# Another order for the opening of an mLSTM-and-feed-forward kernel: later gates loaded second, state copies moved, eight filler products less

## The chip, the cores and the metric

The kernel runs on one core of a Trainium2 chip. Its engines are TensorE (PE, with its weight loads shown as PEld), VectorE (DVE), ScalarE (ACT) and GpSimd (POOL); SyncE (SP) issues most of the transfers. The metric is the device time of one launch in microseconds (us), median of several runs. Before the change it is 528.15 us, the median of three runs from 528.1 to 528.36.

## The reference, cut to what matters

Float32 throughout. An mLSTM cell runs over 768 time steps for 4 batches of 8 heads with 40 dimensions each; its output, reshaped to 3072 rows of 320, passes through a feed-forward block with a gated cosine.

```python
for t in range(S):
    m_new = maximum(f_gate[t] + m, i_gate[t])
    f_stab, i_stab = exp(f_gate[t] + m - m_new), exp(i_gate[t] - m_new)
    C = f_stab * C + i_stab * outer(v[t], k[t])      # 40 x 40 for each head
    n = f_stab * n + i_stab * k[t]
    y[t] = sigmoid(o_gate[t]) * (C @ q[t]) / maximum(abs(n . q[t]), 1)
x = y, as (3072, 320)
h = x @ w_in                                         # (320, 2048)
out = (h * cos(h)) @ w_out                           # (2048, 320)
```

## The kernel before, in words

**Chunks and cells.** The time axis is cut into 6 chunks of 128 steps. A *cell* is one chunk of one batch, n = 4c + b, 24 in all (in the code B is 4, C is 128). Within a cell the recurrence is done by products: a 128 x 128 matrix of decays E for each of 8 heads is multiplied into the scores q.k, and that weighs the values; across chunks a state `st[b]` is carried. Once the four cells of a chunk are done, their outputs stand turned in `xT[c]`, and the feed-forward of these 512 rows can begin: class `Up` (L691 for two blocks of 128 features, L697 for the last 64, kept in `w_in_l`), then `near` (ACT L705), `rest` (DVE L708), `sin` (ACT L713) and `gate` (DVE L717) make h cos h, and the products of L729 and L812 go down through `w_out`.

**Order.** Every engine works through its queue in the order in which the program issues, and the order of the opening is written out by hand in `first_cells`: cells 0 to 3 (all of chunk 0), plus the preparation of cell 4, called B. Then `first_parts(b)` interleaves the cells 4 to 7 with the feed-forward of chunk 0, and `both_parts` goes on so for the later chunks.

**Steps of a cell in the opening.** `load` and `load_E` issue transfers on SP. `wall_in` and `spread` (PE) or, for cells 2 and 3, a load of rows of M from DRAM give the exponents; `decay_exponents` subtracts the gate sums (DVE L415, for halves L421) and for the cells whose E was loaded masks the upper triangle (POOL L416); `decay` is the exponential (ACT L426, L430). `turn` transposes queries and keys (PE L462), `scores` multiplies them (PE L523), `weigh` multiplies scores by E (DVE L529), `values` multiplies with the values (PE L541), `normalize` divides by the denominator (DVE L597 to L605) and leaves y. `weigh_k` (POOL L435) weighs the keys, `seam_u` (PE L652) makes the state's increment `pu` of them, `state` copies it into `st[b]` in four copies (ACT L671), `seam_x` transposes y (PE L637, L639) and `seam_out` copies it into xT (ACT L663). `turn_keys`, `keys_out`, `turn_blocks`, `scale_q` and `odd_values` prepare cell B, whose turned form runs later through `turn_gate` (DVE L501, which transposes the output gate `og` made by `sigmoid(1)`, ACT L338 and L340), vt (PE L554) and `normalize_turned` (DVE L576 to L588).

**Gates.** The gates of chunk 0 (F0, a0) are loaded by `gates_in` and scanned by `gates_first`. The later chunks' gates (F1, a1, 80 KB each) are loaded by `later_gates_in` (L231, L232) and scanned by `gates_sums` (DVE L256), `gates_less_sums` (L259 to L261) and `gates_maxima` (L264, which stores to `M_d[1]`). `gates_exponents` (POOL L271, L272), `gates_exp` (ACT L276, with two POOL stores to `G_d`), `gates_diagonal` (DVE L283), `gates_turn` (PE L291, L292) and `gates_keep` (ACT L297, L300) put the later chunks' gates into the tables `tab` and `fades`.

**Weights.** w_in and w_out come as pairs of 32-bit words that are taken apart on ACT (`take_apart`, L160 and L162) and put together on DVE and POOL (`put_together`, DVE L167, L169, L171, POOL L172), a piece at a time; `pieces` holds those of w_in (a first and a second block of 128 rows, then w_in_l), `outs` those of w_out.

**Fillers.** `warm(k)` issues k products of a zero tile on PE (L895) that nothing reads.

**Tiles.** In the first four cells the PSUM tiles of even cells come from a pool of two buffers (`ps_a`), those of odd cells from one of four (`ps_o`); `ps_u` has two for the two halves of an Up; E has three buffers, so that E(B) takes the buffer of E(0). The tile y and its helper have one buffer each.

Of the kernel before, what the change touches and what calls it, by code (L numbers as in the profile page):

```python
# [29 lines left out]
def kernel(  # L30
# [20 lines left out]
    nc = tc.nc  # L51
# [352 lines left out]
    def psum_o():  # L404
        return ps_o.tile([128, HP, C], FP, name="pm", tag="o")
# [256 lines left out]
            xT[c] = p2.tile([128, NK + 1, B, C], FP, name="xT", tag="xT")  # L662
        nc.scalar.copy(out=xT[c][:, :, b], in_=pxs[n])  # L663

    def state(n):
        if n < N - B:
            for j, r, s, w in halves(n):
                u = increment(n, r, w)
                s = like(s, u)
                if n < B:  # L670
                    nc.scalar.copy(out=s, in_=u)  # L671
                else:
                    nc.vector.tensor_tensor(out=s, in0=s, in1=u, op=OP.add)

# [228 lines left out]
    def first_cells():  # L903
        gates_in()
        nc.scalar.copy(out=ident_b, in_=ident)
        load(0, "qk")
        gates_first()
        fill_raw()
        later_gates_in()
        load(0, "v")  # L910
        load(1, "qk")
        load_o(0, (0, 1))
        load(1, "v")
        load(2, "qk")
        load_E(0)
        load_E(1)
        load_E(2)
        load(2, "v")
        load_E(3)
        load_o(0, (2, 3))  # L920
        load(3)
        pieces.extend(weights_in(0))
        load_two(B, "qk")
        warm(9)
        gates_sums()
        wall_in(0, 1, psum_o())
        wall_in(0, 0, pmu)
        gates_less_sums()
        gates_maxima()
        gates_first_out()  # L930
        turn(0)
        gates_exponents()
        wall_in(1, 0, psum_o())
        spread(0, 0)
        spread(0, 1)
        turn_out(0, False)
        decay_exponents_half(0, 0)
        scores(0)
        decay_exponents_half(0, 1)
        turn(1)  # L940
        decay(0)
        weigh(0)
        spread(1, 0)
        fill_states()
        turn_out(1, False)
        wall_in(1, 1, psum_o())
        decay_exponents_half(1, 0)
        spread(1, 1)
        sigmoid(0, slice(0, 2))
        decay_exponents_half(1, 1)  # L950
        weigh_k(0)
        fill_vr()
        values(0)
        scores(1)
        normalize(0)
        turn(2)
        decay(1)
        decay_exponents(2)
        turn_out(2, False)
        warm(1)  # L960
        seam_u(0)
        load_one(B)
        state(0)
        seam_x(0)
        seam_out(0)
        scores(2)
        weigh(1)
        decay_exponents(3)
        decay(2)
        weigh(2)  # L970
        values(1)
        normalize(1)
        gates_exp()
        load_E(B)
        outs.append((0, weights_out(0)))
        load_E(B + 1)
        load_o(1)
        decay(3)
        turn(3)
        turn_out(3)  # L980
        gates_diagonal()
        sigmoid(0, slice(2, 4))
        values(2)
        seam_x(1)
        seam_out(1)
        take_apart(*pieces[0])
        weigh_k(2)
        scores(3)
        take_apart(*pieces[1])
        normalize(2)  # L990
        take_apart(*pieces[2])
        gates_keep(*gates_turn())
        warm(3)
        weigh(3)
        values(3)
        weigh_k(1)
        seam_u(2)
        seam_x(2)
        seam_out(2)
        put_together(*pieces.pop(0))  # L1000
        pieces.extend(weights_in(1))
        normalize(3)
        seam_u(1)
        load_one(B + 1)
        outs.append((1, weights_out(1)))
        low_dimensions(B)
        seam_x(3)
        seam_out(3)
        turn_keys(B, ps_o, "o")
        keys_out(B)  # L1010
        weigh_k(3)
        put_together(*pieces.pop(0))
        decay_exponents(B)
        turn_blocks(B)
        put_together(*pieces.pop(0))
        state(2)
        seam_u(3)
        decay(B)
        state(1)
        state(3)  # L1020
        weigh_k(B)
        odd_values(B)
        scale_q(B)
        clear_low()
# [21 lines left out]
    def first_parts(b):  # L1046
        n = B + b
        for i in range(2):
# [7 lines left out]
            if i == 0:  # L1056
                scores(n)
                if b == 0:
                    warm(8, psum_o())
                for e in range(2):  # L1060
                    up.near(e)
                for e in range(2):
                    up.rest(e)
                weigh(n)
                if b > 0:
                    decay_exponents(n + 1)
                for e in range(2):
                    up.sin(e)
                if b == 1:
                    take_apart(*pieces[0])  # L1070
                take_apart(*outs[0][1])
                if b == 0:
                    for e in range(2):
                        up.gate(e)
                    turn_blocks(n + 1)
                    next_out()
                    decay_exponents(n + 1)
                    sigmoid(1)
                else:
                    for step in "gw" if b == 1 else "wg":  # L1080
                        if step == "g":
                            for e in range(2):
                                up.gate(e)
                        elif pieces:
                            put_together(*pieces.pop(0))
                            more()
                    next_out()
                    decay(n + 1)
                down_slot(0, f2)
                turn_gate(n)  # L1090
                values(n)
                seam_u(n)
                fade(n)
                normalize_turned(n)
                low_out(n)
                if n == 2 * B - 1:
                    load_two(n + 3, "qk")
                if n > B + 1:
                    load_E(n + 3)
                if b == B - 2:  # L1100
                    load_o(2)
                sin_next()
                if b > 0:
                    if pieces:
                        take_apart(*pieces[0])
                        put_together(*pieces.pop(0))
                        more()
                        take_apart(*pieces[0])
                    take_apart(*outs[0][1])
            else:  # L1110
                if n == 2 * B - 1:
                    load_two(n + 3, "Kv")
                for e in range(2):
                    up.near(e)
                if b == 0:
                    for piece in pieces[0:2]:
                        take_apart(*piece)
                    put_together(*pieces.pop(0))
                    more()
                for e in range(2):  # L1120
                    up.rest(e)
                if b == 0:
                    put_together(*pieces.pop(0))
                    more()
                    load_two(n + 2, "Kv")
                else:
                    state(n)
                for e in range(2):
                    up.sin(e)
                    up.gate(e)  # L1130
                weigh_k(n + 1)
                odd_values(n + 1)
                if b == 0:
                    take_apart(*pieces[0])
                    take_apart(*outs[0][1])
                if b == 0:
                    state(n)
                if pieces:
                    put_together(*pieces.pop(0))
                    if b == 0:  # L1140
                        load_two(n + 2, "q")
                    more()
                if n == B + 1:
                    low_dimensions(n + 1)
                if b == 0:
                    decay(n + 1)
                else:
                    turn_blocks(n + 1)
                    if b < B - 1:
                        turn_keys(n + 1)  # L1150
                        keys_out(n + 1)
                next_out()
                scale_q(n + 1)
                down_slot(0, f2)
                if b == 0:
                    turn_keys(n + 1)
                    keys_out(n + 1)
                    hold(9)
                if b == 1:
                    load_two(n + 3)  # L1160
                if b < 2:
                    load_E(n + 3)
                if b == 1:
                    take_apart(*pieces[0])
                if b == B - 1:
                    weight_sums(0)
# [110 lines left out]
```

## Time and profile before

| what | value |
|---|---|
| median of three runs | 528.15 us (528.1 to 528.36) |
| profiled execution, its time | 527.42 us |
| profiled execution, its span | 525.5 us |
| PE busy | 511.2 us |
| DVE busy | 413.0 us |
| ACT busy | 284.4 us |
| POOL busy | 248.2 us |
| granted PE clock | 1.00 |

The span is the time from the first to the last instruction of the profiled execution; 1.92 us lie around it, and that execution is 0.73 us shorter than the median. The busy times add up to more than the span because the engines run beside one another. In a line of a timeline the first number is the start in us from the span's start, the second is how long the group took, "x8" is how many instructions it groups, and the bracket tells how long the engine had been idle and what it had waited for. In a line of the waits the numbers are the total, how often, and the longest.

The opening, by stages of 5 us, with the busy time of each engine in it:

| stage, us | PE | DVE | ACT | POOL |
|---|---|---|---|---|
| 5 to 10 | 5.00 | 4.09 | 2.25 | 0.63 |
| 10 to 15 | 5.00 | 3.77 | 3.61 | 4.85 |
| 15 to 20 | 4.22 | 4.40 | 4.64 | 3.34 |
| 20 to 25 | 4.98 | 3.25 | 4.46 | 3.89 |
| 25 to 30 | 5.00 | 4.79 | 4.36 | 0.36 |
| 30 to 35 | 4.19 | 4.13 | 3.15 | 2.29 |
| 35 to 40 | 4.48 | 3.28 | 4.72 | 3.55 |
| 40 to 45 | 3.95 | 2.58 | 4.87 | 3.10 |
| 45 to 50 | 5.00 | 4.21 | 4.95 | 0.98 |
| 50 to 55 | 5.00 | 4.86 | 4.42 | 3.98 |
| 55 to 60 | 3.93 | 4.92 | 4.18 | 3.25 |

### The profile page before, as it was taken

How to read it: one execution, taken by the hardware profiler on the slowest of the kernel's cores; microseconds unless marked ns; L12 is line 12 of the kernel's file. 1: busy time of each engine (PE TensorE's matmuls, PEld its weight loads, DVE VectorE, ACT ScalarE, POOL GpSimd, SP SyncE). 2: the span in 40 equal slices, each digit the busy share in tenths (PEclk: the TensorE clock that was granted, in tenths of full speed). 3: DMA queues.
4: the chain of work that ended last, by engine and by line, in shares of the span. 5: the costliest groups of instructions: out<-in, count | busy, mean ns of one | idle time of the engine just before them, and what ended most of it. 6: DMA issues, size and time to landing. Idle time of an engine off the chain costs nothing.

```text
span 525.5 us, 10532 instructions
## 1 busy us (share of the span) xinstructions
PE 511.2 (97%) x3864; PEld 342.4 (65%) x3864; DVE 413.0 (79%) x921; ACT 284.4 (54%) x540; POOL 248.2 (47%) x398
## 2 busy tenths in 40 slices
PE   9999899999999999999999999999999999999996
PEld 6864455555666667666766666676576676666756
DVE  5887998986887887897887898788798878664636
ACT  4979897773953654752652843644745531322221
POOL 6745665544587687355356344444434334121211
PEclk9999999999999999999999999999999999999999
DMA  8898998999266475266357167348110000000001
GB/s 165 212 242 202 282 207 224 181 248 164 95 138 102 97 159 77 71 158 104 97 116 121 53 133 147 85 99 150 41 57 6 1 6 6 26 25 1 0 1 50
DMA packets 96978, 57.15 MB, mean 109 GB/s; under 512 B 62272, under 2 KB 89008, under 8 KB 96928
## 3 DMA queue, kind: packets, MB, share of 16 engines
q1 hardware_dynamic: 95152, 54.66, 48.2%
q0 software_dynamic: 1392, 1.48, 1.2%
q8 instruction: 30, 0.49, 0.4%
q10 hardware_dynamic: 384, 0.36, 0.2%
q14 instruction: 20, 0.16, 0.1%
HBM read 51.05 MB, written 4.11 MB: 105 GB/s over the span
## 4 chain that ended last, share of the span: by engine, by line
PE 79%; ACT 9%; DVE 7%; DMA 2%; issue 2%; POOL 0%; ACTq 0%; SPq 0%; DVEq 0%; POOLq 0%
PE pup L691 28%; PE acc L812 22%; PE pup L697 8%; PE po L729 4%; PE ps L523 3%; PE late L812 2%; ACT E L430 2%; DMA o<-in_o_gate_dram 2%; DVE n L708 1%; PE ph L541 1%; PE pu L652 1%; PE vt L554 1%; ACT L430 1%; ACT L338 1%; PE vt L567 1%
## 5 line engine op out<-in xcount | busy, mean ns | idle before, releaser
L691 PE MATMUL pup<-xT,w_in_sb 128*128 128x512 f32 x384 | 175.8, 601 | 2.5 <-DVE g L717 2.5
L705 ACT ACTIVATE n<-pup 128x512 int32<-128x512 f32 x96 | 53.8, 595 | 195.2 <-PE pup L697 135.3
L708 DVE SCALAR_TENSOR_TENSOR n<-pup,n 128x512 f32<-128x512 f32 x96 | 63.2, 687 | 82.3 <-ACT n L705 80.7
L691 PEld LDWEIGHTS pup<-xT,w_in_sb 128*128 128x128 f32 x384 | 69.7, 190 | 88.8 <-issue 80.3
L771 POOL TENSOR_TENSOR D<-g 128x128 f32<-128x128 f32 x40 | 19.6, 490 | 152.8 <-DVE g L717 138.6
L713 ACT ACTIVATE n<-n 128x512 f32<-128x512 f32 x96 | 59.3, 630 | 14.0 <-DVE n L708 14.0
L717 DVE SCALAR_TENSOR_TENSOR g<-pup,n 128x512 f32<-128x512 f32 x96 | 62.1, 683 | 1.8 <-ACT n L713 0.2
L812 PE MATMUL acc<-w_out_sb,g 128*128 128x160 f32 x320 | 58.5, 304 | 0.0
L812 PE MATMUL acc<-T,g 128*128 128x160 f32 x320 | 57.9, 301 | 0.1
L697 PE MATMUL pup<-xT,w_in_l 64*128 64x512 f32 x192 | 54.3, 641 | 0.5 <-POOL w_in_l L172 0.5
L812 PEld LDWEIGHTS acc<-w_out_sb,g 128*128 128x128 f32 x320 | 47.9, 190 | 5.4 <-issue 3.9
L812 PEld LDWEIGHTS acc<-T,g 128*128 128x128 f32 x320 | 48.2, 190 | 3.4 <-issue 2.7
L430 ACT ACTIVATE E<-E,tab 128x128 f32<-128x128 f32 x160 | 49.0, 388 | 0.4 <-POOL E L416 0.2
L729 PE MATMUL po<-w_out_sb,g 128*128 128x320 f32 x128 | 36.4, 437 | 1.3 <-POOL w_out_sb L172 1.3
L812 PE MATMUL acc<-T,S 128*128 128x160 f32 x160 | 34.9, 300 | 0.0
L589 POOL TENSOR_TENSOR yt<-yt,db 128x128 f32<-128x128 f32 x20 | 11.1, 553 | 48.5 <-DVE db L584 48.5
L523 PEld LDWEIGHTS ps<-t,t 40*128 40x128 f32 (+1 forms) x384 | 25.2, 188 | 11.6 <-issue 7.4
L529 DVE TENSOR_TENSOR E<-ps,E 128x512 f32<-128x512 f32 x48 | 30.7, 681 | 2.0 <-ACT E L426 1.1
L729 PEld LDWEIGHTS po<-w_out_sb,g 128*128 128x128 f32 x128 | 23.7, 190 | 12.3 <-POOL w_out_sb L172 1.7
L697 PEld LDWEIGHTS pup<-xT,w_in_l 64*128 64x128 f32 x192 | 14.6, 185 | 24.1 <-issue 20.8
L812 PE MATMUL acc<-w_out_sb,S 128*128 128x160 f32 x160 | 28.8, 299 | 0.0
L812 PEld LDWEIGHTS acc<-T,S 128*128 128x128 f32 x160 | 26.3, 190 | 2.7 <-issue 2.7
(192 smaller groups left out, 905.9 us busy)
## 6 DMA issues: line engine op xcount, KB each, us to landing
E<-M_d SPq DMA_DIRECT2D x22, 512.0 KB
qr<-in_q_dram SPq DMA_DIRECT2D x36, 160.0 KB
G<-G_d SPq DMA_DIRECT2D x20, 256.0 KB
bits<-in_moe_w_out_dram SPq DMA_DIRECT2D x8, 640.0 KB
kr<-in_k_dram SPq DMA_DIRECT2D x32, 160.0 KB
bits<-in_moe_w_in_dram SPq DMA_DIRECT2D x32, 128.0 KB
out_dram<-o_sb SPq DMA_DIRECT2D x22, 160.0 KB
o<-in_o_gate_dram SPq DMA_DIRECT2D x40, 80.0 KB
```

What stands on the lines that cost most here:

```text
L430: nc.scalar.activation(out=Es[n][:, h], in_=Es[n][:, h], func=AF.Exp, scale=-1.0, bias=tab[:, c, 0, g:g + 1])
L523: nc.tensor.matmul(ps[j][:, p], kT[r, p], qT[r, p], start=True, stop=True)
L529: nc.vector.tensor_tensor(out=w, in0=pss[n][j], in1=w, op=OP.mult)
L691: nc.tensor.matmul(pu, w_in_sb[:, i, ts(2 * f2 + e, 128)], x(i), start=(i == 0 and not low_first), stop=(i == NK - 1 and low_first))
L697: nc.tensor.matmul(pu, w_in_l[r, f2], x(NK, r), start=low_first, stop=not low_first)
L705: nc.scalar.activation(out=self.n[e], in_=self.pu[e], func=AF.Copy, bias=0.25)
L708: nc.vector.scalar_tensor_tensor(out=self.n[e].bitcast(FP), in0=self.pu[e], scalar=0.25, in1=self.n[e], op0=OP.add, op1=OP.subtract)
L713: nc.scalar.activation(out=r, in_=r, func=AF.Sin, scale=TWO_PI_DOWN)
L717: nc.vector.scalar_tensor_tensor(out=g, in0=self.pu[e], scalar=TWO_PI, in1=self.n[e].bitcast(FP), op0=OP.mult, op1=OP.mult)
L729: nc.tensor.matmul(po[c][b], gs[c, f][:, ts(b, C)], w_out_sb[:, f], start=(f == 0), stop=(f == NF - 1))
L771: tt(out=D1, in0=G0[:, 1, 1], in1=G1[:, 1, 1], op=OP.add)
L812: nc.tensor.matmul(a, lhs, rhs, start=start, stop=stop)
```

## The change

No arithmetic changes and no tile changes. `state` takes the copying instruction as an argument, and the steps of `first_cells` are written in another order:

- SP issues the loads of F1 and a1 second and third, ahead of the queries and keys of cell 0; the rest of its order is as it was.
- DVE runs the later gates' scans before it does anything for cell 0's decays, and has decay_exponents(2) ahead of normalize(0) and weigh(1); in the order before it came behind normalize(0).
- POOL has weigh_k(0) and weigh_k(1) before the states are filled, weigh_k(2) ahead of the conversion of the first weights and weigh_k(3) between the first and the second piece; the mask of E(B) (decay_exponents(B)) precedes the additions (L172) of w_in's second piece and of w_in_l, where it stood between them.
- ACT runs the gates' exponentials right behind decay(1), gates_keep ahead of the first take_apart, and takes w_in_l apart ahead of w_in's second piece. Of the twelve state copies L671 that stood between seam_out(3) and near, those of cell 1 come right behind seam_out(1), those of cell 2 go to DVE, and those of cell 3 come in `first_parts`, behind half a piece of w_out and ahead of sigmoid(1).
- PE issues spreads, turns, scores and seams in another order, and 4 fillers in place of 12 besides the nine at the start (warm(1), warm(3), warm(8) become warm(1), warm(3)).

```diff
-    def state(n):
+    def state(n, copy=nc.scalar.copy):
...
-                    nc.scalar.copy(out=s, in_=u)
+                    copy(out=s, in_=u)
...
         gates_in()
         nc.scalar.copy(out=ident_b, in_=ident)
+        later_gates_in()
         load(0, "qk")
         gates_first()
         fill_raw()
-        later_gates_in()
...
         gates_sums()
+        gates_less_sums()
+        gates_maxima()
         wall_in(0, 1, psum_o())
         wall_in(0, 0, pmu)
-        gates_less_sums()
-        gates_maxima()
+        gates_exponents()
+        spread(0, 1)
         gates_first_out()
+        spread(0, 0)
+        decay_exponents_half(0, 0)
         turn(0)
-        gates_exponents()
+        decay_exponents_half(0, 1)
+        wall_in(1, 1, psum_o())
+        spread(1, 1)
         wall_in(1, 0, psum_o())
-        spread(0, 0)
-        spread(0, 1)
+        spread(1, 0)
         turn_out(0, False)
-        decay_exponents_half(0, 0)
+        weigh_k(0)
+        weigh_k(1)
+        fill_states()
+        decay(0)
         scores(0)
-        decay_exponents_half(0, 1)
+        decay_exponents_half(1, 0)
         turn(1)
-        decay(0)
         weigh(0)
-        spread(1, 0)
-        fill_states()
-        turn_out(1, False)
-        wall_in(1, 1, psum_o())
-        decay_exponents_half(1, 0)
-        spread(1, 1)
         sigmoid(0, slice(0, 2))
         decay_exponents_half(1, 1)
-        weigh_k(0)
-        fill_vr()
+        turn_out(1, False)
+        decay(1)
         values(0)
+        gates_exp()
         scores(1)
+        decay_exponents(2)
         normalize(0)
         turn(2)
-        decay(1)
-        decay_exponents(2)
         turn_out(2, False)
-        warm(1)
+        seam_x(0)
         seam_u(0)
         load_one(B)
-        state(0)
-        seam_x(0)
-        seam_out(0)
-        scores(2)
-        weigh(1)
-        decay_exponents(3)
-        decay(2)
-        weigh(2)
-        values(1)
-        normalize(1)
-        gates_exp()
         load_E(B)
         outs.append((0, weights_out(0)))
+        weigh(1)
+        gates_diagonal()
+        values(1)
         load_E(B + 1)
         load_o(1)
+        seam_out(0)
+        state(0)
+        decay_exponents(3)
+        normalize(1)
+        fill_vr()
+        decay(2)
+        scores(2)
+        turn(3)
         decay(3)
-        turn(3)
+        weigh_k(2)
+        pg = gates_turn()
         turn_out(3)
-        gates_diagonal()
+        scores(3)
+        weigh(2)
+        gates_keep(*pg)
+        values(2)
+        take_apart(*pieces[0])
         sigmoid(0, slice(2, 4))
-        values(2)
+        take_apart(*pieces[2])
         seam_x(1)
-        seam_out(1)
+        seam_u(1)
+        put_together(*pieces.pop(0))
+        weigh_k(3)
+        seam_u(2)
         take_apart(*pieces[0])
-        weigh_k(2)
-        scores(3)
-        take_apart(*pieces[1])
-        normalize(2)
-        take_apart(*pieces[2])
-        gates_keep(*gates_turn())
-        warm(3)
         weigh(3)
         values(3)
-        weigh_k(1)
-        seam_u(2)
+        warm(1)
+        normalize(2)
+        seam_out(1)
+        state(1)
         seam_x(2)
         seam_out(2)
-        put_together(*pieces.pop(0))
         pieces.extend(weights_in(1))
         normalize(3)
-        seam_u(1)
         load_one(B + 1)
         outs.append((1, weights_out(1)))
         low_dimensions(B)
+        turn_keys(B, ps_o, "o")
         seam_x(3)
+        seam_u(3)
+        decay_exponents(B)
+        put_together(*pieces.pop(0))
+        put_together(*pieces.pop(0))
         seam_out(3)
-        turn_keys(B, ps_o, "o")
         keys_out(B)
-        weigh_k(3)
-        put_together(*pieces.pop(0))
-        decay_exponents(B)
         turn_blocks(B)
-        put_together(*pieces.pop(0))
-        state(2)
-        seam_u(3)
         decay(B)
-        state(1)
-        state(3)
+        state(2, nc.vector.tensor_copy)
         weigh_k(B)
...
                 if b == 0:
-                    warm(8, psum_o())
+                    warm(3, psum_o())
...
                 take_apart(*outs[0][1])
                 if b == 0:
+                    state(B - 1)
                     for e in range(2):
                         up.gate(e)
```

## The prediction

> **What bounds the kernel now.** I read the busy shares first, then the chain that ended last, then PE's waits of the first 60 us, since the diff touches only the opening (it re-orders the steps for the first four cells and one step of the pass after them).
>
> ```profile
> span 525.5 us, 10532 instructions
> ...
> PE 511.2 (97%) x3864; PEld 342.4 (65%) x3864; DVE 413.0 (79%) x921; ACT 284.4 (54%) x540; POOL 248.2 (47%) x398
> ...
> PE 79%; ACT 9%; DVE 7%; DMA 2%; issue 2%; POOL 0%; ACTq 0%; SPq 0%; DVEq 0%; POOLq 0%
> ```
>
> PE is busy 97% of the span and carries 79% of the chain, so 21% of the chain, some 110 us, does not run on PE. PE's waits in the first 60 us:
>
> ```profile
> PE pup L691 <- DVE g L717: 1.1, 1, 1.1
> ...
> PE px L637 <- DVE y L605: 0.8, 1, 0.8
> ...
> PE pup L697 <- POOL w_in_l L172: 0.5, 1, 0.5
> ```
>
> No wait of PE in the list of the whole span is longer than 1.3 us, and past 60 us PE shows tenths of 9 in nearly every slice, so an offset that stands at the third Up (the wait of 1.1 us, which ends at 58.83) stays to the end. The question is when that Up starts. Followed back in the timelines, engine by engine (start, duration, engine, line):
>
> ```profile
> 35.41 3.70 PE L691 MATMUL pup<-xT,w_in_sb 128*128 128x512 f32 x8
> 39.63 1.13 PE L697 MATMUL pup<-xT,w_in_l 64*128 64x512 f32 x4 [0.52 <-POOL w_in_l L172]
> ...
> 41.58 1.90 PE L895 MATMUL pm<-nil 128*128 128x512 bf16 x8
> ...
> 44.40 0.42 PE L554 MATMUL vt<-E,vs 128*32 128x128 f32 x8 [0.92 <-issue]
> ```
> ```profile
> 40.24 1.52 ACT L671 COPY st<-pu 40x128 f32<-40x128 f32 x8
> 41.79 1.09 ACT L705 ACTIVATE n<-pup 128x512 int32<-128x512 f32 x2
> ...
> 48.10 1.06 ACT L338 ACTIVATE og<-o 128x1024 f32<-128x1024 f32 x1
> 49.06 0.51 ACT L340 ACTIVATE og<-o 128x128 f32<-128x128 f32 x2
> ```
> ```profile
> 16.98 1.22 DVE L415 TENSOR_TENSOR E<-E,tab 128x1024 f32<-128x1024 f32 x1
> ...
> 32.51 1.19 DVE L605 TENSOR_TENSOR y<-yo,dn 128x256 f32<-128x256 f32 x2 [0.26 <-PE px L639]
> ...
> 42.41 1.29 DVE L708 SCALAR_TENSOR_TENSOR n<-pup,n 128x512 f32<-128x512 f32 x2 [4.07 <-ACT n L705]
> ...
> 49.60 0.88 DVE L501 STREAM_TRANSPOSE oT<-og 128x384 f32<-128x384 f32 x1 [0.72 <-ACT og L340]
> ```
> ```profile
> 32.24 1.03 POOL L435 TENSOR_TENSOR kw<-ks,tab 128x512 f32<-128x512 f32 x1
> 35.35 1.29 POOL L172 TENSOR_TENSOR w_in_sb<-w_in_sb,bits 128x512 int32<-128x512 int32 x1 [2.08 <-ACT xT L663]
> 36.59 1.15 POOL L416 TENSOR_SCALAR_AFFINE_SELECT E<-E 128x1024 f32<-128x1024 f32 x1
> 38.84 0.73 POOL L172 TENSOR_TENSOR w_in_l<-w_in_l,bits 128x256 int32<-128x256 int32 x1 [1.10 <-ACT E L430]
> ```
>
> DVE's transpose L501 waited for ACT's output gate L340. From 49.60 on DVE runs without a gap through vt, yt, two weight pieces and the gate product L717 (57.99) to the Up at 58.83. ACT has no long gap from near (L705, 41.79) to the end of L340 (49.57), 7.78 us: near, a table load, sin, half a w_out piece, a table load, sigmoid. Near itself stood behind eight state copies L671 (40.24 to 41.76), although by the start of 39.63 and 1.13 for four, PE had the first two products of L697 done at about 40.2. So the set chain is near, og, L501, the third Up, and near waits for copies.
>
> **Part by part, in the order of the queues.**
>
> *Later gates.* F1 and a1 (80 KB each) go from 4th and 5th on SP to 2nd and 3rd. F1's scan L256 started at 5.78 after 1.84 us of waiting; DVE's work before it (the memset L219) ends at 4.49, so the scan moves by at most 1.3 us and I take 1.2. The scans, the wall and E(0) come that much earlier: E(0)'s exponent at 10.1 instead of 11.36. It buys nothing, because PE is busy for 5.00 of 5.00 us in both stages 5:10 and 10:15, and spreads, turn and scores(0) still stand in series ahead of values(0) (13.58 before, some 13.5 after). Bounds: 0 to 1.2 us gained. I take 0, nearest to the full stages.
>
> *decay_exponents(2) ahead of normalize(0).* DVE meets L415 with its load E(2) still under way; by the trace's semaphore events that lands at 15.94. DVE, done at about 14.5, idles some 1.5 us; L415 takes 1.22 (to 17.2), and normalize(0), which starts at 15.50 before, starts at 17.2: 1.7 later. Behind it in the queue stand weigh(1), and on PE the key half of turn(2) and seam_x(0). The weights and values of the four cells then follow with PE nearly full. Walking the queues with the durations of before puts the first Up at 35.2 to 35.5 against 35.41. k(B) lands at 32.98 and holds PE's turn_keys in both orders. So most of the 1.7 us goes into waits that were there (0.63 at seam_u(0), 0.81 at px, 0.92 ahead of vt) and into fillers. Cost 0 here; if the cover fails, see the last rival.
>
> *Keys away from products of two SBUF tiles.* Two L605 take 0.56 us alone (16.50) and 1.34 and 1.19 beside POOL's key product L435 (24.45, 32.51), each ending with it: 0.78 + 0.63 = 1.4 us of DVE. The first stands beside a full PE; the second made PE wait 0.81 before the first Up. Gain 0 to 0.6 at the first Up, nothing at the third, since by the next item the first Up is no longer what ends last. [...]
>
> *Mask of E(B) ahead of piece 1 on POOL.* Now L416 of decay_exponents(B) precedes L172 of piece 1. It waits for E(B) (issued at 30.60, landing at 35.87 by the semaphore events): 35.95 to 37.1, then L172 37.1 to 38.4 against 36.64. Queued behind it are L172 of w_in_l and the next key product; PE waits for both weights: L691's second block starts no earlier than 38.4, and L697 comes at about 40.2 to 41.3. Near can start at about 41.0. That is a cost of some 0.7 us against what the weights allowed before.
>
> *State copies.* Twelve L671 of 0.19 us (0.75 for four) leave ACT's path ahead of near: state(1) moves up into ACT's slack, state(2) to DVE, which idles 4.07 us before its first L708 and hides four copies, state(3) behind half a w_out piece. Eight of these stood straight before near, 1.52 us. Near moves from 41.79 to 41.0: 0.75 gained, not 1.5, since the weights arrive later. State(3)'s four copies, 0.56 to 0.75, now stand between near and the sigmoid, so og ends at 41.0 + 7.78 + 0.56 = 49.34 against 49.57: 0.2 gained. If ACT's wait for the w_out bits has slack the copies are partly hidden, and walking the queues gives up to 0.6. I take 0.35. L501 follows at once: DVE would be free at 48.9.
>
> *Fillers.* 12 become 4: 8 x 0.22 = 1.8 us of PE. Before, the group at 41.58 ends at 43.5 and PE then idles 0.92 before vt; that at 28.7 stands before values that wait for weigh. They fill waits: 0. ACT's table and gate steps, and POOL's G_d stores (80 KB, earlier, into a DMA lull around 18 to 21), move within slack: 0, at most 0.3 of E(B).
>
> **Sum.** 0 + 0 + 0 + 0.7 lost and 1.5 regained at near, 0.56 lost behind it, less up to 0.4 hidden: -0.35 us. On the profiled execution, 527.42 us (525.5 span and 1.92 around it): 527.07. The median of the runs, 528.15, lies 0.73 above it; with it, 527.8. A measurement of this kernel can tell about 0.2%, 1.06 us, from no change, so the likeliest is "the same".
>
> **Rivals.**
>
> *PE is the bound (faster, 526.4).* Then the fillers count in full: -1.75. For it: 97% and 79%. Against: the idle 0.92 and 0.52 beside them. Chance 0.12.
>
> *E(B) lands earlier (faster, about 527.0).* If the stores and the gate loads out of the crowd bring E(B) 0.9 us forward, POOL's cost of 0.7 vanishes, near starts at 40.1, and og ends 1.7 - 0.56 = 1.1 earlier. For: POOL sets L697, and the mask is set by that landing alone. Against: SP's order from there on is unchanged and the DMA share is about 1.0 from 30 to 40 us. Chance 0.22.
>
> *The wait at L415 comes through (slower, 529.3).* normalize(0) starts 1.7 late, its L605 collides with L416 for another 1.1, and nothing absorbs it: the first Up starts 2.8 late, at 38.2. Up has 1.7 us of room while POOL's piece 1 is late, to about 36.7; beyond it every us moves near one for one: 1.5 - 0.35 = +1.15. It decides from a first Up at 36.7, and the gain is gone at 37.05. For: DVE, POOL and PE all have that step early in their queues. Against: 0.63, 0.81 and 1.0 of slack in between. Chance 0.22.
>
> *It does not do what it says.* [...] Time then as forecast, since that L605 was hidden: 0.04, beside 0.40 for the forecast itself.
>
> **How the numbers follow.** The forecast's own range, 527.3 to 528.3, comes from a net of -0.8 to +0.2. The rivals stretch it: down to 526.3 for the fillers, up to 529.5 for the wait. Faster by over 0.2%: 0.12 + 0.18 of the second rival + 0.07 of the forecast's tail = 0.37. Slower: 0.18 of the third + 0.06 for a load that comes late = 0.24. The rest, 0.39, is within.
>
> **What would show it.** Right: L256 at about 4.6; L415 waiting near 15 for its load and normalize(0) at about 17.2; L416 of E(B) at about 36 and L172 of piece 1 behind it; near at about 41.0 right behind PE's L697; no copies ahead of it; L501 some 0.35 us earlier and still released by ACT's og; the third Up at about 58.5. Wrong: near before 40.4 (the second rival), the first Up after 36.7 (the third), L501 released by DVE's own queue, an offset at the third Up that later stages do not keep, or a granted clock under 1.00 in a stage with fewer fillers.

## The result, and the profile after

The median of the changed kernel is 531.24 us (20 runs, 528.01 to 538.66) against 527.84 us for the kernel before (20 runs, 527.31 to 529.82): 0.64% slower by the medians. The ratio is 1.0052, with a 95% interval of 1.0041 to 1.0063; it leaves out the slowest group of runs below as disturbed (the ratios further down do so too), although here the groups are themselves the effect of the change. The runs are not spread evenly: 1 run at 528.0 us, 12 from 530.4 to 531.4, and 7 from 536.9 to 538.7. The mean granted PE clock of these runs is 1.00 in the first, 0.988 to 0.994 in the second group and 0.971 to 0.976 in the third.

The profiled execution is of the third group (538.66 us). Its page:

```profile
span 536.9 us, 10510 instructions
...
PE 520.9 (97%) x3856; PEld 352.1 (66%) x3856; DVE 414.6 (77%) x925; ACT 284.1 (53%) x536; POOL 248.2 (46%) x398
...
PEclk9656999999999999999999999999999999999999
...
PE 78%; ACT 9%; DVE 8%; issue 2%; POOL 1%; SPq 1%; DMA 1%; ACTq 0%; DVEq 0%; POOLq 0%
```

PE executes eight products less and yet is busy 9.7 us longer. The row PEclk, all 9 before, has 6, 5, 6 in its second to fourth slice: between about 13 and 54 us the clock was down. Cut into stages (the third number from the right is the granted clock):

```profile
core 0: us, PE busy (x) PEld busy (x) DVE busy (x) ACT busy (x) POOL busy (x), PEclk, DMA share, GB/s
...
15.00:20.00 5.00, 2.08 (x16) 1.35 (x12) 3.75 (x7) 3.72 (x6) 3.08 (x6) 0.78 0.84 215
20.00:25.00 5.00, 4.86 (x36) 4.44 (x37) 2.65 (x5) 3.33 (x8) 2.16 (x5) 0.50 1.05 204
...
40.00:45.00 5.00, 5.00 (x25) 4.14 (x25) 1.50 (x7) 0.59 (x2) 0.82 (x1) 0.50 0.91 190
45.00:50.00 5.00, 5.00 (x29) 2.97 (x28) 4.85 (x10) 4.18 (x10) 2.70 (x3) 0.65 0.58 144
50.00:55.00 5.00, 4.17 (x27) 1.95 (x25) 2.04 (x6) 3.64 (x9) 2.85 (x4) 1.00 0.83 176
```

Cut finer, the clock falls at 17.82 and is back at 48.54, 30.72 us later, about nine times 3.41. At half clock PE is full from 25 to 45 us, and with it everything waits: the first Up starts at 47.02, 11.6 us later than before. What stands ahead of the fall is in PE's timeline and DVE's:

```profile
15.34 0.66 PE L462 MATMUL pt<-ident,qs 128*128 128x128 f32 x4
18.35 1.08 PE L462 MATMUL pt<-ident,ks 128*128 128x128 f32 x4 [2.35 <-issue]
20.14 0.66 PE L637 MATMUL px<-ident,y 128*128 128x128 f32 x2 [0.70 <-DVE y L605]
```
```profile
16.14 1.23 DVE L415 TENSOR_TENSOR E<-E,tab 128x1024 f32<-128x1024 f32 x1 [2.67 <-DMA E<-M_d]
...
18.28 1.84 DVE L605 TENSOR_TENSOR y<-yo,dn 128x256 f32<-128x256 f32 x2
```

PE idles 2.35 us at the key half of turn(2), which needs the PSUM buffer that normalize(0) frees, and again 0.70 us until y(0) is there. DVE had waited 2.67 us at L415 for E(2), with normalize(0) queued behind it. In the stretch of 3.41 us that ends at the fall (14.41 to 17.82) PE is busy for 1.59 us.

### The profile page after: what moved, and what is told of

It reads as the page before. It is cut to its first block, busy times and chain, and to the rows that moved or that the text cites. A ratio compares the mean times of both kernels' runs of the same rounds, so it can differ in the third digit from the quotient of the medians.

```text
span 536.9 us, 10510 instructions
## 1 busy us (share of the span) xinstructions
PE 520.9 (97%) x3856; PEld 352.1 (66%) x3856; DVE 414.6 (77%) x925; ACT 284.1 (53%) x536; POOL 248.2 (46%) x398
## 4 chain that ended last, share of the span: by engine, by line
PE 78%; ACT 9%; DVE 8%; issue 2%; POOL 1%; SPq 1%; DMA 1%; ACTq 0%; DVEq 0%; POOLq 0%
PE pup L691 28%; PE acc L812 22%; PE pup L697 8%; PE po L729 4%; PE ps L523 3%; PE late L812 2%; PE ph L541 2%; ACT E L430 2%; PE pu L652 2%; DVE n L708 1%; PE vt L554 1%; ACT L338 1%; PE vt L567 1%; ACT og L338 1%; DVE g L717 1%
## 5 line engine op out<-in xcount | busy, mean ns | idle before, releaser
L691 PE MATMUL pup<-xT,w_in_sb 128*128 128x512 f32 x384 | 176.6, 602 | 3.1 <-DVE g L717 3.1
L691 PEld LDWEIGHTS pup<-xT,w_in_sb 128*128 128x128 f32 x384 | 69.9, 191 | 89.9 <-issue 81.6
L812 PE MATMUL acc<-w_out_sb,g 128*128 128x160 f32 x320 | 58.5, 304 | 0.0
L697 PE MATMUL pup<-xT,w_in_l 64*128 64x512 f32 x192 | 54.3, 641 | 0.0
L523 PEld LDWEIGHTS ps<-t,t 40*128 40x128 f32 (+1 forms) x384 | 26.5, 199 | 11.1 <-issue 7.4
L529 DVE TENSOR_TENSOR E<-ps,E 128x512 f32<-128x512 f32 x48 | 30.7, 681 | 0.5 <-PE ps L523 0.5
L697 PEld LDWEIGHTS pup<-xT,w_in_l 64*128 64x128 f32 x192 | 14.6, 184 | 23.5 <-issue 21.6
L523 PE MATMUL ps<-t,t 40*128 40x128 f32 (+1 forms) x384 | 28.0, 288 | 0.3
```

Of the source, the lines that this page charges most:

```text
L523: nc.tensor.matmul(ps[j][:, p], kT[r, p], qT[r, p], start=True, stop=True)
L529: nc.vector.tensor_tensor(out=w, in0=pss[n][j], in1=w, op=OP.mult)
L691: nc.tensor.matmul(pu, w_in_sb[:, i, ts(2 * f2 + e, 128)], x(i), start=(i == 0 and not low_first), stop=(i == NK - 1 and low_first))
L697: nc.tensor.matmul(pu, w_in_l[r, f2], x(NK, r), start=low_first, stop=not low_first)
L812: nc.tensor.matmul(a, lhs, rhs, start=start, stop=stop)
```

## The experiments

The theory: PE's idle time in the opening, made by L415 standing ahead of normalize(0), lets the granted clock fall to 0.50 for several us, and that is the whole loss. The rivals: the late chain itself (y(0) and the collision of L605), the fillers that were taken out, or PE as the bound. In the table, *falls* counts the runs with a mean granted clock under 0.995, that is about two or more stretches of 3.41 us at half clock (3.41 is the shortest time that the clock is down in a profile, 39.05 to 42.46 in e9); *one stretch* counts those from 0.995 to 0.997, since the profiles of e9 (0.996) and e7 (0.997) have one such stretch each. The runs of the kernel before that went with these experiments have 7 falls and 10 runs with one stretch among 116.

| kernel | median, us | before beside it | ratio (95% interval) | falls | one stretch |
|---|---|---|---|---|---|
| changed kernel | 531.24 | 527.84 | 1.0052 (1.0041 to 1.0063) | 19 of 20 | 0 |
| e9, changed kernel again | 530.76 | 527.98 | 1.0026 (0.9997 to 1.0055) | 10 of 12 | 1 |
| e1, 15 fillers added | 527.97 | 527.85 | 1.0001 (0.9992 to 1.0010) | 0 of 11 | 0 |
| e5, 10 of them | 527.85 | 528.10 | 0.9995 (0.9978 to 1.0011) | 0 of 12 | 1 |
| e6, the other 5 | 528.13 | 528.10 | 1.0003 (0.9989 to 1.0018) | 0 of 12 | 3 |
| e14, 4 of the 10 | 527.53 | 527.58 | 0.9985 (0.9961 to 1.0009) | 1 of 12 | 1 |
| e2, L415 put back | 527.31 | 527.85 | 0.9986 (0.9972 to 0.9999) | 0 of 12 | 1 |
| e12, filler counts of before | 535.00 | 527.98 | 1.0102 (1.0041 to 1.0164) | 6 of 6 | 0 |
| e13, gate loads put back | 532.75 | 527.58 | 1.0035 (0.9999 to 1.0071) | 9 of 12 | 1 |
| e7, 16 fillers after the fall | 534.75 | 528.10 | 1.0105 (1.0072 to 1.0137) | 4 of 6 | 1 |
| e3, before with L415 first | 528.21 | 527.85 | 1.0008 (0.9997 to 1.0019) | 0 of 11 | 1 |
| e4, before with few fillers | 528.52 | 527.85 | 1.0012 (0.9996 to 1.0028) | 2 of 12 | 6 |
| e8, e2 and piece 1 first | 527.59 | 528.10 | 0.9983 (0.9964 to 1.0002) | 1 of 12 | 5 |
| e10, e8 and fillers | 527.21 | 527.98 | 0.9979 (0.9952 to 1.0006) | 1 of 12 | 4 |
| e11, before, copies moved | 527.23 | 527.98 | 0.9990 (0.9964 to 1.0016) | 0 of 12 | 2 |

### e1: PE's two gaps filled

```diff
-    def turn(n):
+    def turn(n, fill=0):
...
         for src in (qs(n), ks(n)):
+            if pts[n]:
+                warm(fill)
...
-        turn(2)
+        turn(2, 10)
...
+        warm(5)
         seam_x(0)
```

> The changed kernel with 15 more filler products on PE: 10 between the query half and the key half of turn(2), where PE idled from 16.0 to 18.35 us, and 5 ahead of seam_x(0), where it idled from 19.43 to 20.14. Theory (clock): PE idles too long here, its granted clock falls to 0.5 for a stretch of several us and the opening takes longer; with the fillers the clock stays at 1.00 in every run, the levels of 531 and 537 us vanish, and the time is 527.3 to 528.2 (0 to -0.1% against before), with the same late y(0). Rival (late chain): the cost is the late normalize(0) and the collision of L605 with the mask L416 (1.28 us on DVE), which the fillers leave in place; then the time stays at about 531 and the levels remain.

527.97 us, no falls. In its profile DVE's L605 still takes 2.01 us beside the mask L416 and y(0) is as late as in the changed kernel, but PE is full:

```profile
17.02 2.32 PE L897 MATMUL pw<-nil 128*128 128x512 bf16 x10
...
36.13 1.98 PE L693 MATMUL pup<-xT,w_in_sb 128*128 128x512 f32 x4 [0.24 <-ACT xT L665]
...
59.36 1.96 PE L693 MATMUL pup<-xT,w_in_sb 128*128 128x512 f32 x4 [1.67 <-DVE g L719]
```

(The edit shifts line numbers by two: L897 is the filler, L693 the Up.) Adding work to PE takes 3.3 us off the median. The late chain is still there: the third Up is at 59.36 against 58.83. That is one profile of each, and e6's, with the same late normalize(0), has 58.38, so what the late chain costs is not settled; it is far from 3 us. Theory held, the late-chain rival fell.

### e5, e6 and e14: which gap, and how much of it

e5 has only `turn(2, 10)`, e6 only `warm(5)` ahead of seam_x(0), e14 only `turn(2, 4)`.

> The changed kernel with only the 10 fillers between the query half and the key half of turn(2), where PE idled 2.35 us. Theory: that wait, made by DVE's wait for E(2) ahead of normalize(0), is what lets the clock fall; clock 1.00 in nearly all runs and 527.7 to 528.3. Rival (it takes both gaps, or the later one of 0.70 us): levels of 531 and more stay in half of the runs.

> The changed kernel with only 5 fillers ahead of seam_x(0), in the later gap of 0.70 us. Theory (the first gap decides): the clock falls as in the changed kernel, by the trace at about 18 us, before these fillers run; median 530.5 to 532 with levels at 531 and 537. They may bring the clock back earlier, so fewer runs at 537. Rival (the later gap decides): clock 1.00, about 528.

> The changed kernel with 4 fillers (0.9 us) in place of 10 between the halves of turn(2). Theory (the fall hangs on how much of a stretch of 3.41 us PE idles; the wait of 1.5 to 2.4 us is shortened to 0.6 to 1.5 and the gap of 0.7 to 1.1 behind it stays): fewer falls than the changed kernel, but more than with 10: between a tenth and a half of the runs at 530 or more. Rival (any filler in the gap resets it): none. Rival (it takes the whole gap): as the changed kernel, nine tenths.

e5 behaved as expected. e6 did not: I expected the clock to fall before those five fillers run, with a median of 530.5 to 532, and no run lost two stretches; three, at 0.996 and 0.997, fit one; the time is that of the rival. So either group of fillers is enough to keep the median at that of before. Whether the first gap alone would let the clock fall is not shown, because in e6's profile that gap is only 0.64 us:

```profile
17.87 0.63 PE L462 MATMUL pt<-ident,ks 128*128 128x128 f32 x4 [0.64 <-PE pt L462]
```

The program up to there is that of the changed kernel; why the gap differs is told further down. With 4 fillers (0.9 us, e14) one run in twelve is down (0.977) and one more loses about one stretch (0.996); that is at the low end of what I expected and close to the rival that any filler suffices.

### e2: the step put back

```diff
-        decay_exponents(2)
         normalize(0)
         turn(2)
+        decay_exponents(2)
```

> The changed kernel with one step put back: decay_exponents(2) behind normalize(0) and turn(2), as in the kernel before. Nothing waits for E(2)'s load on DVE ahead of y(0). Theory (clock): PE's idle time between 16 and 20 us shrinks to under 1 us in one piece, the clock stays at 1.00, time 526.9 to 528. Rival (the removed fillers leave the clock open elsewhere): drops remain, some runs at 530 or more.

527.31 us, no falls: moving this one step repairs the kernel, and it is 0.14% under the kernel before. In its profile PE still idles 1.90 us in one piece (ahead of seam_x(0)), more than I expected, and the clock stays. At 1.00 the profile shows what the rest of the change is worth; PE, ACT and DVE in turn:

```profile
37.98 1.98 PE L691 MATMUL pup<-xT,w_in_sb 128*128 128x512 f32 x4 [1.35 <-POOL w_in_sb L172]
...
58.68 1.53 PE L691 MATMUL pup<-xT,w_in_sb 128*128 128x512 f32 x3 [1.66 <-DVE g L717]
```
```profile
41.05 1.08 ACT L705 ACTIVATE n<-pup 128x512 int32<-128x512 f32 x2 [2.07 <-PE pup L697]
```
```profile
49.46 0.88 DVE L501 STREAM_TRANSPOSE oT<-og 128x384 f32<-128x384 f32 x1 [1.33 <-ACT og L340]
```

### e3 and e4: the two suspects alone in the kernel before

e3 puts decay_exponents(2) ahead of normalize(0) in the kernel before. e4 drops `warm(1)` ahead of seam_u(0) and makes 3 into 1 and 8 into 3.

> The kernel before with that one step alone: decay_exponents(2) ahead of normalize(0). normalize(0) moves from 15.5 to about 17.2 and PE waits some 1 us at the key half of turn(2), with one filler and the waits of before around it. Theory (clock): the idle time is about half of that in the changed kernel (there 2.35 + 0.70), so the clock may fall in some runs, not in most: median 527.8 to 529. Rival (the step alone makes it): the levels of 531 and 537 show as often as in the changed kernel.

> The kernel before with the changed kernel's filler counts: the filler at 17.41 us left out, 3 become 1 at 28.7, 8 become 3 at 41.6; nothing is moved. Theory (clock falls by the wait at L415): PE is busy enough, clock 1.00, time 527.4 to 528.1, no change. Rival (fillers hold the clock): granted clock under 1.00 in many runs, 530 or more. Rival (PE is the bound): 526.1.

e3: no falls. DVE waits only 0.34 us at L415 there, but L415 itself takes 1.93 us, so normalize(0) starts at 17.10, as late as in the changed kernel; PE idles 1.32 us at the key half of turn(2), and the first Up comes 0.54 us later (35.95). 528.21 us lies in the expected range. So the step alone, in the order of before, does not make the clock fall; it takes something else of the change with it. e4: the theory that PE is busy enough without them is wrong in part. The median moves by 0.7 us, two runs are at 532.2 and 537.8, and six more fit one lost stretch (0.996 and 0.997): 8 of 12 against 17 of 116 before. Its profile, that of the run at 532.2, shows falls at 21.4 (back at 28.3) and at 48.8 (back at 52.2), each close behind a place where fillers had been. So the fillers do hold the clock. The rival that PE is the bound (526.1) fell: with eight products less nothing is gained.

### e12 and e13: what else the fall needs

e12 is the changed kernel with the filler counts of before (one ahead of seam_u(0), 3 and 8); e13 has `later_gates_in()` back behind `fill_raw()`.

> The changed kernel with the filler counts of before: one ahead of seam_u(0), three at the place of its one, eight in first_parts. The wait at L415 stays. Theory (the wait at turn(2)'s key half lets the clock fall; one filler of 0.22 us cannot fill 2.35 us): the levels of 531 and 537 stay in most runs. Rival (the fillers that were removed are the cause): clock 1.00 in most runs, 528.

> The changed kernel with the loads of F1 and a1 put back to 4th and 5th on SP; all else as changed, decay_exponents(2) ahead of normalize(0) too. Theory (two parts make the gap: values(0) comes 1.2 us earlier, and y(0) is tied to E(2)'s landing at about 15.9): the scan L256 starts at 5.8 again, values(0) at about 13.6, PE's wait at turn(2)'s key half shrinks from 1.5 to 2.4 us to about 0.7 to 1.1, and most runs keep the clock: median 527.5 to 528.5, at most a quarter of the runs at 530 or more. Rival (the wait at L415 alone makes it in this order of the queues): the groups at 531 and 537 hold most runs.

e12: all six runs fall, so the missing fillers are not the cause in the changed kernel; the wait is, as e2 showed, and one filler behind it does not help. In its profile the clock falls at 18.44 and is back at 28.68:

```profile
15.00:20.00 5.00, 2.63 (x26) 1.81 (x24) 4.05 (x8) 3.83 (x6) 3.08 (x6) 0.84 0.84 215
20.00:25.00 5.00, 5.00 (x36) 4.13 (x37) 2.31 (x4) 3.22 (x7) 2.50 (x6) 0.50 1.04 209
25.00:30.00 5.00, 5.00 (x39) 4.46 (x38) 2.25 (x8) 0.72 (x2) 0.73 (x1) 0.63 0.81 205
30.00:35.00 5.00, 5.00 (x78) 4.59 (x76) 4.60 (x11) 4.93 (x10) 1.90 (x2) 1.00 1.22 241
```

e13: my theory fell. The scan starts at 5.98 again, and PE's gaps shrink to 1.00 and 0.72 us, but 9 of 12 runs fall all the same (in its profile from 19.93 to 40.41). The early gate loads are not needed for it. What besides L415 is needed, since e3 does not fall, is not found.

### e7: dense products after the fall

```diff
         decay(2)
+        warm(16)
         scores(2)
```

> The changed kernel with 16 fillers between decay(2) and scores(2), at about 25 us, well behind the fall of the clock. In the changed kernel's profile the clock stays at 0.50 from 18.0 to 48.5 us although PE is busy 5.00 of 5.00 us in each stage from 25 to 45. Theory (it is dense products that bring the clock back, not a busy PE): the clock comes back at about 30, no run near 537; the fillers themselves cost 3.5 us at full clock and up to 7 at half, so 531 to 535, all runs in one group. Rival (the length of a fall does not hang on the work): runs at 537 plus the fillers' price, 540 and more.

530.03 to 535.61 us, none near 540, so the rival fell; but the runs are not one group as expected, and four of six, at 0.989, fit three stretches. In its profile the clock falls at 21.7, the 16 fillers start at 22.95, and it is back at 25.1. That agrees with dense products bringing it back. It does not show that only they do: in e12 and e13 the clock came back among scores and values.

### e8 and e10: the mask of E(B), and all together

e8 is e2 with

```diff
-        decay_exponents(B)
         put_together(*pieces.pop(0))
+        decay_exponents(B)
         put_together(*pieces.pop(0))
```

and e10 is e8 with `warm(9)` ahead of seam_x(0) and 8 fillers again in first_parts.

> The changed kernel with decay_exponents(2) behind normalize(0) and turn(2), and with put_together of w_in's second piece ahead of decay_exponents(B), so that POOL converts piece 1 (L172) before it waits for the load of E(B) at its mask L416. Theory (the term of 0.7 us: the mask ahead of the weights holds near): against the run with decay_exponents(2) put back alone (527.31), PE's wait of 1.35 us at L691's second block goes, near moves from 41.05 to about 39.9, and the time falls by 0.8 to 1.2: 526.1 to 526.5. Rival (the DMA or ACT's exponential L430 holds near anyway): near at 40.8 or later and 527.0 to 527.5.

> Both edits of e8 (decay_exponents(2) behind normalize(0); w_in's second piece ahead of the mask of E(B)), with 9 fillers ahead of seam_x(0), where PE still idled 0.95 to 1.9 us, and the group in first_parts at 8 as in the kernel before. Theory: the late group of e8 (528 to 529.6 at clocks of 0.994 to 0.997) goes, what is left is its low group: 525.3 to 526.5, 0.3% to 0.45% under the kernel before. Rival (the fillers delay y(0)'s seam and so the first Up): 527 or more, clock 1.00.

e8 in its profile, ACT:

```profile
38.25 2.45 ACT L430 ACTIVATE E<-E,tab 128x128 f32<-128x128 f32 x8 [1.32 <-POOL E L416]
40.60 1.05 ACT L705 ACTIVATE n<-pup 128x512 int32<-128x512 f32 x2
```

PE's wait at L691 is gone, but near moves by 0.45 us only (41.05 to 40.60), because the mask now comes later and ACT's exponential behind it holds near: the rival was right about the place, though 40.60 is a little under its 40.8. The runs spread from 525.27 to 529.59, and with the fillers of e10 from 525.64 to 530.15. The best runs are 2 us under the kernel before, the medians 0.5 and 0.8 us, and both intervals take in no change; the expected end of the late runs did not come. I cannot call either faster.

### e11: the state copies alone

The kernel before, with state(1) behind seam_u(1), state(2) on DVE and state(3) in first_parts.

> The kernel before with the state copies alone moved as in the change: cell 1's earlier on ACT (behind seam_u(1)), cell 2's to DVE, cell 3's behind half a w_out piece. POOL's order is that of before, so L697 has its weights at 39.6. Theory: near starts at about 40.3 instead of 41.79 (-1.5), the four copies ahead of the sigmoid give 0.6 to 0.75 back, og and the third Up come 0.75 to 0.9 us earlier: 526.9 to 527.2. Rival (something else sets the third Up): no change, 527.6 to 528.1.

```profile
40.81 1.08 ACT L705 ACTIVATE n<-pup 128x512 int32<-128x512 f32 x2 [0.57 <-PE pup L697]
```
```profile
49.23 0.89 DVE L501 STREAM_TRANSPOSE oT<-og 128x384 f32<-128x384 f32 x1 [1.33 <-ACT og L340]
```
```profile
58.46 1.96 PE L691 MATMUL pup<-xT,w_in_sb 128*128 128x512 f32 x4 [1.68 <-DVE g L717]
```

Near is 0.98 us earlier, not 1.5, since L697 is done only at 40.8; L501 and the third Up are 0.37 us earlier. The median is 0.75 us under its neighbour, but the ratio, 0.9990 (0.9964 to 1.0016), takes in no change.

### e9: the changed kernel again

> The changed kernel unaltered, on the same chip as the three kernels beside it, as their yardstick and for a profile at another level of the clock. Theory: nearly all runs with a granted clock under 0.995, in the two groups near 531 and 537. The profile should show falls and rises at distances that are whole multiples of about 3.41 us, as in the profiles so far (17.91 to 48.55 in the changed kernel; 21.44 to 28.3 and 48.8 to 52.1 in the kernel before with fewer fillers; 21.7 to 25.1 with the dense fillers). Rival (the two groups are another disturbance of the chip): the group near 531 shows no fall in the opening.

One run at 527.7, seven from 529.7 to 531.3, four from 537.6 to 538.3: the groups are a property of this program. This profile has its fall elsewhere, from 39.1 to 42.5, during a second gap that the change makes:

```profile
34.86 1.98 PE L691 MATMUL pup<-xT,w_in_sb 128*128 128x512 f32 x4 [0.24 <-ACT xT L663]
39.62 3.38 PE L691 MATMUL pup<-xT,w_in_sb 128*128 128x512 f32 x4 [2.78 <-POOL w_in_sb L172]
```

PE waits 2.78 us for piece 1, which POOL converts behind the mask of E(B); that mask waited for its load until 37.23. So the wait at L415 is not the only place where this kernel can lose the clock. Nor is all that this run lost the clock's: one stretch loses 1.7 us at most, and the run, 530.21, is 2.2 over 528.0.

## Why the prediction was wrong

**The step that failed** is the pricing of *decay_exponents(2) ahead of normalize(0)*, "Cost 0 here". The delay itself was foreseen: normalize(0) at 17.2 (17.29 measured), L415 waiting for a load that lands at about 16, L605 colliding with the mask (1.84 us for two instead of 0.56, 1.28 more; in the profiles of e6, e13 and e14 the two do not meet and L605 takes 0.56). But PE's idle time was priced only by how late it makes the chain, which at full clock is about 0.66 us of median (e1 against e2, 527.97 and 527.31), and not by what it does to the clock. That costs 3.0 us in the middle group and 9.5 in the slow one (medians of 531.0 and 537.5 against 528.0). The profile of e12 (531.22) has three stretches of 3.41 us at half clock and that of the changed kernel (538.66) nine; 1.7 us are lost in each, of which 1.1 to 1.2 come out in the time (3.2 and 10.7 us over 528.0).

**The gap was also too small.** I expected values(0) at 13.5, since PE was full in two stages; it came at 12.35 in the profile, so the gap was 2.35 us and not some 1.5. But 13.5 is right for some executions, and which one a profile catches is luck. PE's first products run at half clock (in the profile before nine fillers from 0.99 take 4.02 us, eight from 41.58 take 1.90), and the moment when the clock comes up differs from one execution to the next. The same product, first in the profile before, then in that of the changed kernel:

```profile
4.81 0.63 PE L394 MATMUL pm<-wall,ident_b 128*128 128x512 bf16 x1
4.50 0.38 PE L394 MATMUL pm<-wall,ident_b 128*128 128x512 bf16 x1
```

In the profile of the kernel before, the clock came up at 6.99 us and values(0) started at 13.58. In the changed kernel, e7, e9 and e12 it came up at 4.2 to 4.9 us, values(0) started at 12.35 to 12.71, and the first gap was 1.53 to 2.35 us; in e1, e5, e6 and e14, with the same program up to the query half of turn(2), values(0) started at 13.5 to 13.7, and in e14 eight products L401 still take 1.56 us at 5.66 (1.05 at 9.47), so the clock came up during or after them. So the openings of two profiles here are not like for like, and the counts of runs are the better evidence.

**Fillers at 0** was half right: taking them out gains nothing (e4), so they fill waits, but they also hold the clock, and without them the kernel before falls in 2 runs of 12 and loses one stretch in 6 more. A fall of the clock was named among the things that would make the prediction wrong; no rival and no chance stood for it.

**The slower rival** had the right place, L415, and the wrong mechanism: with the clock held the first Up comes at 34.2 (e14) to 36.1 (e1), so its point of decision, 36.7, is not reached. No run shows the 1.1 us that its sum takes for L605 beside L416; the changed kernel's profile shows 1.28 (1.84 against 0.56 for the two).

**What held, at full clock.** L256 at 4.52 (4.6 foreseen); near at 41.05 right behind L697 (41.0); L501 released by ACT's og at 49.46; the third Up at 58.68 (58.5). The sum of -0.35 us is -0.15 at the third Up in e2 and -0.37 in e11, but these are single profiles: in e1, e5, e6 and e14 the third Up lies anywhere from 58.38 to 59.73, so neither settles the term. The mask of E(B) was rightly a cost: 1.35 us of PE's wait in e2. Two readings were off without consequence: the memset L219 that ends at 4.49 is POOL's and not DVE's, and each pair of L605 beside the key product ends 0.43 us after it, not with it.

**What the profiles show of the clock.** It is 0.50 or 1.00, and the distances from fall to return are 30.7 (changed kernel), 20.5 (e13), 10.2 (e12), 6.8 (e4) and three times 3.4 us (e4, e7, e9), whole multiples of 3.41. In the changed kernel it fell after a stretch with PE busy 1.59 of 3.41 us, and with PE busy 5.00 of 5.00 us in each stage from 25 to 45 us it stayed at 0.50.

**What stays open** is what makes the clock fall and return. PE's busy share does not sort the cases. In steps of 3.41 us, counted in each profile from a change of the clock, stretches with 1.59, 1.66, 1.70 and 2.27 us busy (changed kernel, e12, e13 and e4, to 21.44) were followed by a fall, and stretches with 1.76 and 2.09 (e9, to 18.57, and e3, to 18.40) were not. A weighted count sets the fall in the changed kernel apart from the kernel before. It is an estimate worked out afterwards from PE's instructions in the profiles of before, the changed kernel and e13, and no run was made to test it. Give each product the time that its columns take at full clock (0.22 us for 512 of bf16, 0.46 for 512 of f32, from the timelines), times its weights as a share of 128*128 (64*128 is half). In the changed kernel the stretch that ends in the fall then has 1.33 us, the eight behind it at half clock have 0.87 to 1.31, and the ninth, which ends in the return, has 1.49; in the kernel before no whole stretch from 6.99 us on has less than 1.40, and the clock stays. In e13 the fall follows a stretch with about 1.2, but its return at 40.41 one with about 1.0, against the count. By it the small f32 products weigh little, although the profile shows PE as full.

Why e3 does not fall while e13, with gaps of 1.00 and 0.72 us, does is not settled by any run. The filler that e3 keeps ahead of seam_u(0) is a candidate; e12 has one there too, with a longer wait, and falls.

## What to carry to other kernels

Look for every place where a re-ordering makes a busy PE wait a microsecond or two, and price it twice: once for the lateness, and once for the clock, which here cost about five to fourteen times as much (3.0 and 9.5 us against 0.66). Before removing products that nothing reads, look at the granted clock of many runs, not at one profile: groups of run times with a mean clock under 1.00, here 3.0 and 9.5 us above the rest, are the mark of it. And keep an instruction that waits for a load out from in front of the one that frees PE's next buffer.

## What the runs showed of the hardware that was not expected

The clock, once down, stayed at 0.50 through 20 us of small float32 products on a PE that the profile shows as full; with sixteen 128x512 bf16 products (e7) it was back in 3.4 us. And 0.9 us of such products (e14), or 1.1 us in another gap (e6), kept all but one of 24 runs from losing more than one stretch, where the changed kernel without them kept 1 of 20.
